# A network piece between the off-diagonal and the state products: a new order of pieces in an HGRN2 + PReLU network kernel

## The chip, the cores and the metric

One core of one Trainium2 chip. The metric is the device time of one execution in microseconds. Before the change three runs took 632.31, 633.37 and 634.52 us; the median is 633.37. A step of such a kernel is made of instructions on five engines that each run in their own order: TensorE (PE; its weight loads are shown apart as PEld), VectorE (DVE), ScalarE (ACT), GpSimd (POOL) and SyncE (SP, which here only starts DMA transfers).

## What is computed

```python
for t in range(S):                                   # HGRN2, for each of B=4 batches and H=8 heads, D=48
    state = f[t, :, None] * state + k[t, :, None] * v[t, None, :]      # f = sigmoid(f_logit)
    y[t] = q[t] @ state
x = y as (B*S, H*D)                                  # 3072 tokens x 384
h = x @ w_in                                         # 384 -> 2048
g = maximum(h, 0) + alpha * minimum(h, 0)
out = g @ w_out                                      # 2048 -> 384
```

All in 32-bit floats; S is 768.

## The kernel before

The sequence is cut into NC = 6 chunks of C = 128 time steps, and the four batches into two pairs. One *step* of the kernel is one chunk of one pair: 12 steps, in the order of `steps` (L725), the chunk being the outer loop. A step's attention gives 256 tokens, which the network then takes in the next step. So step n runs, side by side, the attention of step n, the network of step n−1 and the preparation of step n+1.

Each of these is a generator, and each `yield` ends a *piece*. A string says in which order pieces are issued (L753 to L756): a letter names the generator, a number repeats it.

- `P`, `Q` (`prepare`, L261): the decays of a chunk and the scaled forms of q and k. `P` is this step's own, `Q` the next step's. Five pieces: sigmoid, copies and the lagged products (L282 to L298); four ScalarE copies us<-qd (L317) and VectorE's two scans (L320, L322); q4 and k4 (L324, L350); kh, ks, q3 (L371, L377); the transposed ks and its 16 small DMAs to `ksn` (L404, L430), with f64 (L417). A sixth copies into `A` and starts the DMAs.
- `O` (`carry`, L435): two pieces. The first is the off-diagonal product `off` (64 matmuls, L447; in the first chunk also 128 of L457 and the transposes pk of L474) and ScalarE's copies of it (L465). The second is the state product `pd` (64 matmuls, L487), which takes `ksn` and `vs`, and VectorE's update of the state, `moved(0)` (L497, L501).
- `S` (`attend`, L511): six pieces. For each of the two batches, `raw` (L523) with its four predicated copies (L529) and `qu` (L538) with its seven (L544; three of L560 in the first chunk). Then ScalarE's copies A<-ad for each batch (L566), then `py` (L577), then the second state update, y and the DMAs that make xT of it (L605).
- `n` (`network`, L611): for the step before. Eight pieces of six matmuls `ph` (L620; fp32, which the trace records as 12), ScalarE's `neg` (L625) and VectorE's two `gate` operations (L627); after the fourth and the eighth also four sums (L701). Then pa and pb, pc and pd, pa and pc again, pe, each eight matmuls (L659), and small VectorE operations (L672 to L686) and the stores. The first step's network is plainer: its second product is `po` (L640).
- `a`, `w` and `b`, `v` (`load_weights`, L168): the weights of the two network products arrive in 8 pieces each; the uppers (`a`, `b`) start the load on SP and run two ScalarE operations (L202, L204), the rests (`w`, `v`) four VectorE operations (L210 to L228; for w_out the last one is an accumulating DMA of POOL, L230).
- `W` (L703): sums of w_out's quarters, which the later networks take.

TensorE, VectorE and ScalarE run in exactly the order in which the pieces issue their instructions (L745). SP and POOL are put in order by a scheduler. Two resources tie the engines together: off, pd, raw, qu, py and pk share two PSUM pairs (`psa`, 2 buffers), so each product waits until the copies of the one before the last are done; ph, pa to pe share four banks (`psn`). `neg` has two buffers. The raw weight pieces have four buffers (RAWS), the uppers three (TOPS).

The code that sets the order:

```python
first = (...)          # one string for each of the first four steps
usual = "S n2 S n2 O2 n Q n2 Q n2 Q S3 n Q S n Q n Q n"
```

In a usual step TensorE's order is thus raw qu, ph0 ph1, raw qu, ph2 ph3, off pd, ph4 to ph7, pa pb, py, pc pd, pa pc, pe. (The names `pd` of L487, the state product, and `pd` of L659, a product of the network, are two different things.)

Of the kernel before, what the change touches and what calls it, by code (L numbers as in the profile page):

```python
# [32 lines left out]
def kernel(  # L33
# [39 lines left out]
    W = U * HP * C  # L73
# [61 lines left out]
    for m in range(1, NB):  # L135
        lo = UO[m] + (4 if m == 1 else 0)
        n = NB - m
# [4 lines left out]
    for half in range(2):  # L142
        for m in range(1, NQ):
            n = NQ - m
# [558 lines left out]
    def halves_of_w_out():  # L703
# [20 lines left out]

    steps = [(bp, c) for c in range(NC) for bp in range(B // U)]  # L725
    first = (
        "P2 a P w P a P a w O P w S a w S Q a S O a w S Q2 w S2",
        "P a w a P w n b w n v O b v n b S v n2 P S b S v n b S v n b v n Q b n Q v b O v Q n v W Q S2 Q W n2 W Q W",
        "O n2 S W n2 S Q S n4 O S n Q2 n Q2 S n S n Q n",
        "S n3 S n Q n2 O Q O n2 S Q S n S Q n Q S Q n3",  # L730
    )
    usual = "S n2 S n2 O2 n Q n2 Q n2 Q S3 n Q S n Q n Q n"
    pieces = {key: part for keys, parts in (("aw", load_weights(w_in_sb, w_in, "w_in")),
                                            ("bv", load_weights(w_out_sb, w_out, "w_out")))
              for key, part in zip(keys, parts)}
# [77 lines left out]
```

## Time and profile before

| | before |
|---|---|
| median of three runs | 633.37 us |
| profiled execution | 634.88 us |
| its span | 633.1 us |
| granted TensorE clock, mean | 0.997 |
| TensorE busy | 593.9 us |
| VectorE busy | 512.0 us |
| ScalarE busy | 249.8 us |
| step 3, first raw to next step's | 160.32 to 208.07 us |
| two usual steps, the sixth and seventh | 255.73 to 303.55 and to 351.50 us |

The profile is of one execution. Its chain of work that ended last, and the costliest groups, are read as follows: an operation's line is its place in the kernel, `out<-in` are the program's names of the tiles, the number after x counts records, and for idle time the last part names what ended it.

```profile
PE 73%; DVE 22%; issue 2%; ACT 1%; DMA 1%; DVEq 0%; ACTq 0%
L620 PE MATMUL ph<-xT,w_in_sb 128*128 128x256 f32 x1152 | 258.4, 383 | 0.0
L627 DVE SCALAR_TENSOR_TENSOR gate<-neg,om,ph 128x256 f32<-128x256 f32 x192 | 82.1, 474 | 40.7 <-ACT neg L625 40.5
L566 ACT COPY A<-ad 32x256 f32<-32x256 f32 x96 | 38.5, 401 | 1.4
```

Matmuls are pipelined: the times at which they end are modelled, and a following group can start up to 0.1 us before the end shown for the one ahead of it. "PEldq" in a view stands for TensorE's sequencer, in records of instructions that the engine itself doesn't execute.

### The profile page before, as it was taken

How to read it: one execution, taken by the hardware profiler on the slowest of the kernel's cores; microseconds unless marked ns; L12 is line 12 of the kernel's file. 1: busy time of each engine (PE TensorE's matmuls, PEld its weight loads, DVE VectorE, ACT ScalarE, POOL GpSimd, SP SyncE). 2: the span in 40 equal slices, each digit the busy share in tenths (PEclk: the TensorE clock that was granted, in tenths of full speed). 3: DMA queues.
4: the chain of work that ended last, by engine and by line, in shares of the span. 5: the costliest groups of instructions: out<-in, count | busy, mean ns of one | idle time of the engine just before them, and what ended most of it. 6: DMA issues, size and time to landing. Idle time of an engine off the chain costs nothing.

```text
span 633.1 us, 19007 instructions
## 1 busy us (share of the span) xinstructions
PE 593.9 (94%) x8188; PEld 529.2 (84%) x8188; DVE 512.0 (81%) x1035; ACT 249.8 (39%) x466; POOL 58.8 (9%) x107
## 2 busy tenths in 40 slices
PE   2357999989999999999999999999999999999997
PEld 2356865879789889889889889889889889889997
DVE  5799999999799788888888888888888888762251
ACT  5595792541263153253253253253253253223110
POOL 9010122001001001001001001001001000000000
PEclk9999999999999999999999999999999999999999
DMA  7845796312323313313313313323323301201000
GB/s 239 279 146 182 195 295 162 58 62 73 78 54 91 79 35 85 75 46 84 72 48 84 76 45 84 68 52 84 66 54 85 61 26 26 48 7 26 26 0 26
DMA packets 70323, 53.57 MB, mean 85 GB/s; under 512 B 47296, under 2 KB 62144, under 8 KB 70240
## 3 DMA queue, kind: packets, MB, share of 16 engines
q1 hardware_dynamic: 57536, 25.37, 15.9%
q0 software_dynamic: 7312, 24.78, 13.6%
q10 hardware_dynamic: 5392, 2.21, 1.7%
q8 instruction: 65, 1.06, 0.7%
q14 instruction: 18, 0.15, 0.1%
HBM read 36.21 MB, written 4.72 MB: 65 GB/s over the span
## 4 chain that ended last, share of the span: by engine, by line
PE 73%; DVE 22%; issue 2%; ACT 1%; DMA 1%; DVEq 0%; ACTq 0%
PE ph L620 34%; PE pc L659 8%; PE pa L659 8%; PE pe L659 4%; PE pd L659 4%; PE pb L659 4%; PE qu L538 3%; PE py L577 3%; PE raw L523 3%; PE pd L487 2%; DVE gate L627 2%; DVE S L701 2%; DVE us L333 1%; DVE qd L290 1%; DVE ad L529 1%
## 5 line engine op out<-in xcount | busy, mean ns | idle before, releaser
L620 PE MATMUL ph<-xT,w_in_sb 128*128 128x256 f32 x1152 | 258.4, 383 | 0.0
L620 PEld LDWEIGHTS ph<-xT,w_in_sb 128*128 128x128 f32 x1152 | 216.7, 190 | 32.3 <-issue 2.4
L625 ACT ACTIVATE neg<-ph 128x512 f32<-128x512 f32 x96 | 57.2, 596 | 187.4 <-PE ph L620 139.6
L627 DVE SCALAR_TENSOR_TENSOR gate<-neg,om,ph 128x256 f32<-128x256 f32 x192 | 82.1, 474 | 40.7 <-ACT neg L625 40.5
L659 PE MATMUL pa<-w_out_sb,gate 128*128 128x192 f32 x352 | 62.0, 329 | 1.8 <-DVE gate L627 1.8
L659 PE MATMUL pc<-t,S 128*128 128x192 f32 x352 | 61.7, 329 | 0.0
L659 PEld LDWEIGHTS pa<-w_out_sb,gate 128*128 128x128 f32 x352 | 57.8, 190 | 3.7 <-issue 1.9
L659 PEld LDWEIGHTS pc<-t,S 128*128 128x128 f32 x352 | 57.3, 190 | 0.6
L529 DVE COPY_PREDICATED ad<-mraw,raw 128x256 f32<-128x256 int32 (+1 forms) x96 | 42.3, 441 | 7.3 <-PE raw L523 4.8
L544 DVE COPY_PREDICATED ad<-mquad,qu 128x224 f32<-128x224 int32 (+6 forms) x140 | 41.9, 299 | 6.2
L422 ACT COPY A<-q 48x512 f32<-48x512 f32 x44 | 27.2, 617 | 42.4 <-DVE q L371 38.4
L566 ACT COPY A<-ad 32x256 f32<-32x256 f32 x96 | 38.5, 401 | 1.4
L333 DVE TENSOR_TENSOR us<-us,fs 128x768 f32<-128x768 f32 (+5 forms) x60 | 36.7, 612 | 0.1
L677 ACT COPY o<-pa 128x192 f32<-128x192 f32 x11 | 3.5, 318 | 75.3 <-PE pa L659 61.5
L290 DVE TENSOR_TENSOR qd<-qd,f 128x768 f32<-128x768 f32 (+2 forms) x36 | 27.1, 753 | 6.1 <-ACT qd L285 6.1
L538 PE MATMUL qu<-us,k 48*32 48x112 f32 (+1 forms) x1536 | 27.1, 259 | 4.2 <-issue 3.0
L701 DVE TENSOR_TENSOR S<-gate 128x512 f32<-128x512 f32 x44 | 30.3, 688 | 0.8
L659 PE MATMUL pe<-w_out_sb,S 128*128 128x192 f32 x176 | 30.5, 327 | 0.3 <-ACT o L677 0.3
L659 PE MATMUL pb<-t,gate 128*128 128x192 f32 x176 | 30.4, 326 | 0.0
L659 PE MATMUL pd<-w_out_sb,S 128*128 128x192 f32 x176 | 30.4, 326 | 0.0
L577 PEld LDWEIGHTS py<-A,vs 128*64 128x64 f32 x768 | 25.7, 145 | 5.5 <-issue 2.8
L577 PE MATMUL py<-A,vs 128*64 128x64 f32 x768 | 28.1, 233 | 2.0 <-ACT vs L503 1.0
(110 smaller groups left out, 743.0 us busy)
## 6 DMA issues: line engine op xcount, KB each, us to landing
w_out_raw<-in_w_out SPq DMA_DIRECT2D x8, 767.8 KB, 5.0
w_in_raw<-in_w_in SPq DMA_DIRECT2D x8, 767.2 KB, 7.1
f<-in_fT POOLq DMA_DIRECT2D x11, 512.0 KB, 4.5
q<-in_qT POOLq DMA_DIRECT2D x11, 512.0 KB, 4.2
k<-in_kT POOLq DMA_DIRECT2D x11, 512.0 KB, 4.6
out<-o SPq DMA_DIRECT2D x24, 192.0 KB, 2.1
vs<-in_v POOLq DMA_DIRECT2D x22, 192.0 KB, 4.3
w_out_sb<-w_out_lead POOLq DMA_DIRECT2D x8, 384.0 KB, 6.3
```

What stands on the lines that cost most here:

```text
L290: nc.vector.tensor_tensor(qdv[d], qdv[d - 1][:, :, :, 1:5 - d], f[:, :, 1:5 - d].rearrange("p (g i) r -> p g i r", i=NB), ALU.mult)
L333: nc.vector.tensor_tensor(us[:, :, UO[m]:UO[m] + 4 * n].rearrange("p g (i r) -> p g i r", r=4), us[:, :, skip:skip + 4 * n].rearrange("p g ...
L529: nc.vector.copy_predicated(adu[:, :, :, d:4], mraw[:, d, :, d:4].bitcast(I32).unsqueeze(1).broadcast_to((128, H, NB, n)), rv[:, :, QO[d]: ...
L538: nc.tensor.matmul(qu[DB * j:DB * (j + 1), par, hp * QS + 4:hp * QS + QL], lhsT=k4[r_, g * DB:(g + 1) * DB], rhs=us[r_, g, 4:QL], start=Tr ...
L544: nc.vector.copy_predicated(ad[:, u, :, :, 4 * m:DB], mquad[:, lo:lo + n].bitcast(I32).unsqueeze(1).unsqueeze(1).broadcast_to((128, 2, HP, ...
L566: nc.scalar.copy(A[s_, u, :, s_], ad[s_, u].rearrange("p r h t -> p (r h) t"))
L577: nc.tensor.matmul(py[64 * par:64 * par + 64, u, o:o + CH], lhsT=vs[bp][:, cc, u, hd * D:hd * D + 64], rhs=A[:, u, par * HP + hp, CH * cc: ...
L620: nc.tensor.matmul(ph[:, j * T:(j + 1) * T], lhsT=w_in_sb[:, kt, m * 128:(m + 1) * 128], rhs=xT[:, kt], start=(kt == 0 and j == 0), stop=( ...
L625: nc.scalar.activation(neg, phv, AF.Relu, scale=-1.0)
L627: nc.vector.scalar_tensor_tensor(gate[:, m % NH, m // NH], neg[:, j], om[:, m:m + 1], phv[:, j], ALU.mult, ALU.add)
L659: nc.tensor.matmul(to[:, 0:DH], lhsT=of(f), rhs=by(f), start=(f == 0 and not more), stop=(f == NH - 1), skip_group_check=True)
L701: nc.vector.tensor_tensor(to, x_, y_, op)
```

## The change

Only the strings change. No instruction is added or removed on TensorE or VectorE.

```diff
     first = (
-        "P2 a P w P a P a w O P w S a w S Q a S O a w S Q2 w S2",
-        "P a w a P w n b w n v O b v n b S v n2 P S b S v n b S v n b v n Q b n Q v b O v Q n v W Q S2 Q W n2 W Q W",
-        "O n2 S W n2 S Q S n4 O S n Q2 n Q2 S n S n Q n",
-        "S n3 S n Q n2 O Q O n2 S Q S n S Q n Q S Q n3",
+        "P2 a P w P a P2 a w a w O a w S2 Q O S Q w S a Q S w S",
+        "P n b P a w a n O b w2 v2 S P b n3 v S b2 S2 v2 n Q b n2 Q O b v b n v2 n v S W Q2 S Q W n Q W n W",
+        "n2 S n W n3 S n2 Q O S n O Q2 S n S Q S n Q2 n2",
+        "S n2 S Q n2 O n O S2 n3 Q2 S n2 S Q n Q n2 Q",
     )
-    usual = "S n2 S n2 O2 n Q n2 Q n2 Q S3 n Q S n Q n Q n"
+    usual = "S n2 S n O n O n Q n3 Q n Q S3 n Q S n Q n Q n"
```

In a usual step two things move:

- The first piece of `O` (off) goes ahead of ph3, and the second (pd) behind it. Before, off and pd followed each other behind ph3.
- The second piece of `Q` (ScalarE's us<-qd copies and VectorE's scans) goes from between ph6 and ph7 to behind ph7 and its sums.

In the first steps all kinds of pieces move. In step 0 the attention's pieces come in pairs and weight pieces spread otherwise; in step 1 the prepare pieces come before weight pieces, the first network piece before the uppers of w_in, and off before the second; in step 2 the network's first pieces come ahead of off; in step 3 a network piece stands between off and pd, which were adjacent on TensorE before. With this the scheduler's orders on SP and POOL change up to there: the first load of w_out comes ahead of the last two of w_in, and loads of k, f and v change places with the accumulating DMAs of w_out.

## The prediction

> **What bounds the kernel now.** I read the page's busy shares and slices first, then the windows cut at the steps' ends, the waits of TensorE, the chain through one usual step, and the timeline of TensorE around the two products that the change moves.
>
> ```profile
> PE 593.9 (94%) x8188; PEld 529.2 (84%) x8188; DVE 512.0 (81%) x1035; ACT 249.8 (39%) x466; POOL 58.8 (9%) x107
> PE   2357999989999999999999999999999999999997
> DVE  5799999999799788888888888888888888762251
> ```
>
> TensorE is full from the fifth slice to the end; VectorE is full in slices three to ten, the start-up. The windows say the same in microseconds (busy time and record count of each engine; the stretches are start-up, steps 1 and 2, one usual step, and the end):
>
> ```profile
> 0.00:62.50 62.50, 31.71 (x847) 27.27 (x849) 50.22 (x94) 38.81 (x62) 20.46 (x53) 1.00 0.66 213
> 62.50:160.32 97.82, 94.33 (x1316) 76.83 (x1304) 94.59 (x180) 50.31 (x89) 13.89 (x18) 0.98 0.52 140
> 303.55:351.50 47.95, 47.84 (x660) 43.37 (x660) 41.36 (x86) 17.95 (x36) 3.39 (x5) 1.00 0.27 67
> 590.40:633.10 42.70, 39.33 (x211) 36.55 (x209) 14.46 (x31) 5.42 (x10) 0.00 (x0) 1.00 0.05 17
> ```
>
> A usual step is 47.84 of 47.95 us TensorE, with VectorE at 41.36. So a usual step gets shorter only if TensorE's own stream does. The waits that TensorE shows lie in the start-up, except a few:
>
> ```profile
> PE off L447 <- DVE q L371: 12.1, 1, 12.1
> PE off L457 <- issue: 4.8, 1, 4.8
> PE off L457 <- DVE us L407: 3.4, 2, 2.8
> PE pa L659 <- DVE gate L627: 1.8, 1, 1.8
> ```
>
> What the waits don't show is inside the busy time. The chain through a usual step (start, length, records), where off and pd follow each other:
>
> ```profile
> 317.95 0.71 PE off L447 x50
> 318.66 0.05 issue
> 318.71 0.72 PE pd L487 x6
> 319.43 0.04 issue
> 319.47 0.89 PE pd L487 x57
> 320.35 10.56 PE ph L620 x48
> ```
>
> Six matmuls of pd take as long as the other 57. Elsewhere in the same run, where pd stands behind a network piece, and where off stands alone before one:
>
> ```profile
> 109.83 0.76 PE L447 MATMUL off<-q,kh 48*32 48x32 f32 x64
> 110.51 5.45 PE L620 MATMUL ph<-xT,w_in_sb 128*128 128x256 f32 x24
> 135.32 0.94 PE L487 MATMUL pd<-vs,ksn 64*48 64x48 f32 x64
> ```
>
> pd is 0.94 us there. The records of pd's line in a usual step name what else it runs:
>
> ```profile
> L487 PEldq EVENT_SEMAPHORE  x9: 51/51/51, 318.4 to 319.4; - x9
> ```
>
> Nine semaphore instructions of 51 ns on TensorE's sequencer, at 318.4 to 319.4, exactly the slow microsecond. In the stretch 133 to 137, around the quick pd, the same view has none: its sequencer had passed them while network matmuls ran.
>
> [...]
>
> **The usual step, part by part.** Nothing is added or removed; TensorE's order goes from "ph2 ph3 off pd ph4" to "ph2 off ph3 pd ph4". Before, from off's start to ph4's start: 320.28 − 317.88 = 2.40 us. After, off alone is 110.51 − 109.83 = 0.68, and pd alone 0.94 less the modelled tail of about 0.07 plus a changeover of about 0.05, some 0.92. Together 1.60; saved 0.80. From pd's start to the next ph the eight usual steps have 1.54, 1.51, 1.57, 1.51, 1.55, 1.54, 1.68 and 1.58, so this step is typical. For cover: ph3 runs 2.66 us and pd's semaphores need 9 × 0.051 = 0.46. Bounds: nothing saved if the sequencer doesn't get ahead through one piece, 0.95 if off too gets cheaper. I take 0.75 for each of eight steps: −6.0.
>
> Waits that could appear. off now comes a network piece earlier and needs the PSUM pair that raw1 had; VectorE's copies of raw1 (L529) end at 314.13 and off would start at 315.2: 1.1 us to spare. pd needs qu1's pair, free at 316.53, and starts at 318.6. VectorE's gate 3 moves 0.7 later; it stood idle 1.37 us before that gate, and behind it wait the sums of L701, moved(0) and gate 4. It then has 0.75 idle before L290 and 2.04 before L672 to absorb it. Behind off's ScalarE copies (1.27) stands neg3, which isn't ready for 2.7 us.
>
> Second, Q's scans (L320, L322) and ScalarE's four us<-qd copies (2.15) go behind gate 7 and neg7. Gate 7 was at 332.58, behind both scans; now it is about 0.7 us sooner against ph7, and pa (2.93 instead of 2.76 us, a wait of 0.17 in seven steps) needn't wait: between 0 and −1.2 for all, I take −0.5. The sums that pc needs end sooner too. The us<-qd copies end at about 332.8, before pa's copy and the 3.33 us of A<-ad copies that py needs, so those don't move. The orders of SP's and POOL's queues change only up to the loads and stores of the first steps; in the usual steps each transfer keeps its place.
>
> **The first four steps.** I replayed the new lists by hand with the durations of before's rows. Step 0: VectorE waited 3.75 us for raw0 at 30.15; a weight piece (L210 to L228, 2.6) now lies there, and the attend copies end at about 37.9 instead of 39.4. In ScalarE's order the second A<-ad copy falls behind an upper pair (1.8), so y stays at about 47.0 and ph0 with it: no gain yet on TensorE, 1.5 less backlog on VectorE. Step 1: the prepare pieces come ahead of weight pieces, so the 2.81 us wait of L457 goes and pk ends near 62.2 instead of 64.8. What is late next is raw0: it needs off's pair, and ScalarE does neg0, one w_out upper, two w_in uppers and neg1 before off's copies; about 2.0 lost. Then gates before po 0.35, and landings of w_out pieces 0.5. The po end comes at 108.0 instead of 109.85. Moved queue entries count: the first w_out load goes to SP ahead of the last two w_in loads (median landing 7.1 us), whose uppers stand ahead of neg1; POOL's k load for step 2 goes ahead of a w_out accumulate. Step 2: the 1.77 us gate wait before pa goes, because the scans no longer stand in front, but VectorE is the bound there (94.59 of 97.82), and I find 0.8 and 0.7 us of waits for it early in step 3. Ahead at the end of step 2: about 2.2. Bounds: 5 gained if VectorE's idle is all filled, 4 lost if an upper arrives late in step 1. In step 3 off and pd were adjacent as well (1.58); separated, −0.75.
>
> Sum: −6.0 − 0.5 − 2.2 − 0.75 = −9.45 us. The profiled execution was 634.88 (span 633.1), 1.5 above the median of 633.37; it would come to 625.4. From the median: 623.9. A replay by hand forgets small waits rather than inventing them, so I give back 0.6: 624.5.
>
> **Rivals.** (a) Separation saves nothing in usual steps: pd is slow because of its shape change behind off, or the sequencer stops at the semaphores all the same. Against it stand 0.94 in step 2 and the clean split of 6 and 57 matmuls. Left would be −2.2 − 0.5: 630.7. (b) The usual steps gain, the start-up gives 3 to 4 us back in place of gaining: ScalarE's in-order queue in step 1, or w_out pieces landing late. For it: VectorE at 97%, no slack. 633.4 − 7.25 + 2.5, about 628.5. (c) Slower: off waits for VectorE's copies of raw1 in every usual step. The price is what they are late beyond 1.1 us; from 2.25 us late (1.1 + 9.2/8) it eats everything, and at 2.7 late it gives 8 × 1.6 − 9.2 = +3.6: 637.0. For it: VectorE runs from 341.26 through the next step's raw1 copies with one gap of 1.08. Against it: that gap is there, and nothing is put into that stretch.
>
> **How the numbers follow.** Forecast 0.70, (a) 0.10, (b) 0.14, (c) 0.06. The range reaches from 620.0 (start-up 5 gained, pa's wait all gone) to 629.6, which takes in most of (b) and leaves out (a) and (c). About 1.9 us, 0.3%, is what a measurement can tell from no change. (a) and (b) are mostly beyond it on the fast side; a little of each isn't. Faster 0.90, within 0.04, slower 0.06.
>
> **What would show it.** In the changed profile: off start to ph start near 0.7, pd near 0.94 with no semaphore instruction inside it, usual steps of about 47.0; pa at 2.76; no L407 wait; ph4 of step 3 about 3 us sooner. Wrong if pd stays near 1.6, if a wait of off for L529 appears, or if the first usual step begins after 208.

## The result, and the profile after

The changed kernel takes 630.9 us in the median (628.54 to 633.09), the kernel before 633.41 (632.15 to 635.04) on the same chip: a ratio of 0.996, interval 0.995 to 0.997. It is faster, by 2.5 us; forecast were 8.9. The profiled execution took 629.98 (span 628.2), 0.9 below its median, while that of before was 1.5 above its own: spans differ by more than medians do.

The page of the kernel after, busy shares, and slices of the clock that TensorE was granted:

```profile
PE 590.1 (94%) x8188; PEld 525.2 (84%) x8188; DVE 512.1 (82%) x1035; ACT 248.7 (40%) x466; POOL 58.5 (9%) x107
...
PEclk9958799999999999999999999999999999999999
```

TensorE's busy time fell by 3.8 us. By the trace's clock records the clock is at half from 32.8 to 49.9 us and from 60.1 to 70.3 us. The kernel before shows a 9 in all slices, but its clock records begin only at 52.59 us, and ahead of them its rows are as slow as at half (the figures stand in the last section); behind them it is at half from 62.8 to 66.2 us. So the second stretch is the one that differs, 10.2 us against 3.4. TensorE's waits, kernel after:

```profile
PE off L457 <- issue: 5.5, 2, 3.8
PE py L577 <- ACT A L566: 4.2, 5, 1.9
...
PE pe L659 <- ACT o L677: 2.4, 1, 2.4
...
PE ph L620 <- DMA xT<-y: 0.9, 1, 0.9
PE off L457 <- DVE us L407: 0.6, 1, 0.6
```

The wait for L407 has shrunk from 3.4 to 0.6 as forecast and the gate wait of pa is gone; a wait of pe in step 2 and one for xT were not in the forecast. Of py's 4.2 us, 3.7 lie in step 0, where the copies A<-ad were forecast to come late, and 0.45 in the first usual step; shorter stops of py in the other usual steps don't appear in this list. Two rows of a usual step of TensorE in the kernel before, then the same step in the kernel after:

```profile
330.75 2.93 PE L659 MATMUL pa<-w_out_sb,gate 128*128 128x192 f32 x16
336.21 2.15 PE L577 MATMUL py<-A,vs 128*64 128x64 f32 x64
```

```profile
313.78 0.76 PE L447 MATMUL off<-q,kh 48*32 48x32 f32 x64
314.46 2.86 PE L620 MATMUL ph<-xT,w_in_sb 128*128 128x256 f32 x12
317.25 0.94 PE L487 MATMUL pd<-vs,ksn 64*48 64x48 f32 x64
318.11 10.63 PE L620 MATMUL ph<-xT,w_in_sb 128*128 128x256 f32 x48
328.58 2.76 PE L659 MATMUL pa<-w_out_sb,gate 128*128 128x192 f32 x16
331.18 2.76 PE L659 MATMUL pb<-t,gate 128*128 128x192 f32 x16
333.87 2.44 PE L577 MATMUL py<-A,vs 128*64 128x64 f32 x64
336.24 2.87 PE L659 MATMUL pc<-t,S 128*128 128x192 f32 x16
```

pd is 0.94 us, and its nine semaphore instructions now run under the network piece, as the records of its line in this stretch say. One of them waits 0.475 us, and ph3 covers that too:

```profile
L487 PEldq EVENT_SEMAPHORE  x9: 51/51/475, 314.4 to 315.8; - x9
```

From the second raw to ph4 it is 318.11 − 309.30 = 8.81 us, against 320.28 − 310.73 = 9.55 before: 0.74 saved in this step. (These are times from start to start. The ends shown overlap the next start by more than the 0.1 us said above: raw at 309.30 lasts 0.92, and qu starts at 309.99.) The mean of the eight usual steps is 8.88 against 9.50, 0.62 saved. pa takes 2.60 from start to start instead of 2.76. But py takes 2.37 instead of 2.07. Sum −0.60; the step is 47.33 instead of 47.95. The mean of seven usual steps is 47.37, before 47.83. ScalarE shows why py got longer, first in the kernel before, then in the same stretch of the kernel after:

```profile
328.85 2.15 ACT L317 COPY us<-qd 128x256 f32<-128x256 f32 x4
331.00 0.60 ACT L625 ACTIVATE neg<-ph 128x512 f32<-128x512 f32 x1
333.93 3.33 ACT L566 COPY A<-ad 32x256 f32<-32x256 f32 x8
```

```profile
329.18 0.60 ACT L625 ACTIVATE neg<-ph 128x512 f32<-128x512 f32 x1 [2.39 <-DVE gate L627]
329.68 2.16 ACT L317 COPY us<-qd 128x256 f32<-128x256 f32 x4
331.63 0.37 ACT L667 COPY Csum<-pa 128x192 f32<-128x192 f32 x1
331.90 3.33 ACT L566 COPY A<-ad 32x256 f32<-32x256 f32 x8
```

Gates 5, 6 and 7 on VectorE, kernel after:

```profile
328.20 2.48 DVE L627 SCALAR_TENSOR_TENSOR gate<-neg,om,ph 128x256 f32<-128x256 f32 x6
```

The neg row in each of the two blocks above is neg7. In the kernel after ScalarE is idle for 2.39 us ahead of it, and the view names a gate as what ended that. Most of this is TensorE's own time, as ph7 ends, by the model, only at 318.11 + 10.63 = 328.74; the gate's share is some 0.4 us, from there to 329.18. `neg` has two buffers, and gate 5, the first of these three, must free one. The copies us<-qd now stand behind neg7, and the A<-ad copies behind them end at 335.23: py's records stop inside its second batch, from 334.92 to 335.28, for the last of them. In the kernel before, neg7 starts at 331.00, right behind ph7, which ends at 320.28 + 10.63 = 330.91.

### The profile page after: what moved, and what is told of

It reads as the page before. It is cut to its first block, busy times and chain, and to the rows that moved or that the text cites. A ratio compares the mean times of both kernels' runs of the same rounds, so it can differ in the third digit from the quotient of the medians.

```text
span 628.2 us, 19015 instructions
## 1 busy us (share of the span) xinstructions
PE 590.1 (94%) x8188; PEld 525.2 (84%) x8188; DVE 512.1 (82%) x1035; ACT 248.7 (40%) x466; POOL 58.5 (9%) x107
## 3 DMA queue, kind: packets, MB, share of 16 engines
q8 instruction: 65, 1.06, 0.8%
## 4 chain that ended last, share of the span: by engine, by line
PE 64%; DVE 17%; ACT 10%; issue 4%; DMA 3%; ACTq 1%; DVEq 0%; SPq 0%
PE ph L620 26%; PE pc L659 9%; PE pa L659 6%; PE pe L659 5%; PE pd L659 5%; PE qu L538 3%; ACT A L566 3%; PE raw L523 3%; DVE S L701 3%; DVE gate L627 3%; DVE qd L290 3%; PE py L577 2%; ACT us L317 2%; DMA xT<-y 2%; PE po L640 2%
## 5 line engine op out<-in xcount | busy, mean ns | idle before, releaser
L620 PE MATMUL ph<-xT,w_in_sb 128*128 128x256 f32 x1152 | 262.2, 385 | 0.9 <-DMA xT<-y 0.9
L529 DVE COPY_PREDICATED ad<-mraw,raw 128x256 f32<-128x256 int32 (+1 forms) x96 | 42.3, 441 | 3.1 <-PE raw L523 0.6
L659 PEld LDWEIGHTS pe<-w_out_sb,S 128*128 128x128 f32 x176 | 28.8, 190 | 2.7 <-ACT o L677 2.7
```

What stands on the lines that cost most here:

```text
L529: nc.vector.copy_predicated(adu[:, :, :, d:4], mraw[:, d, :, d:4].bitcast(I32).unsqueeze(1).broadcast_to((128, H, NB, n)), rv[:, :, QO[d]: ...
L620: nc.tensor.matmul(ph[:, j * T:(j + 1) * T], lhsT=w_in_sb[:, kt, m * 128:(m + 1) * 128], rhs=xT[:, kt], start=(kt == 0 and j == 0), stop=( ...
L659: nc.tensor.matmul(to[:, 0:DH], lhsT=of(f), rhs=by(f), start=(f == 0 and not more), stop=(f == NH - 1), skip_group_check=True)
```

## The experiments

All times are medians, each kernel beside runs of the kernel before on the same chip (633.4 to 634.2 there). "Steps 0 to 3" are the four strings of `first`.

**The two halves of the change.** e1 takes from the change's diff only the line of `usual`, e2 only the four of `first`.

> The first four orders of before, the usual order of the change. Theory A (the usual steps gain 0.5 us each net: 0.7 from the separated state product less about 0.3 of py waiting for the copies A<-ad; the start-up gave back): 629.4, that is 4.0 below before. Rival (the usual order's gain needs the new first steps too, or the usual order also carries the loss): 631 or more.

> The first four orders of the change, the usual order of before. Theory A: the new first steps lose 0 to 2 us, 633.4 to 635, since medians left 1.5 us unaccounted for after 8 x 0.5. Rival (start-up is neutral or better, as the one profile with step 4 beginning 0.9 us sooner says): 632.5 or less. The granted clock should fall below 0.99 if the new start-up is what lowers it.

e1: 629.62, ratio 0.9939 (0.9922 to 0.9955). e2: 635.11, ratio 1.0019 (1.0008 to 1.003). So the usual steps gain 4.0 us, and the first four lose 1.5.

**The two halves of the usual step.**

e3 sets only off and pd apart, e4 only puts the second prepare piece later; both against before:

```diff
-    usual = "S n2 S n2 O2 n Q n2 Q n2 Q S3 n Q S n Q n Q n"
+    usual = "S n2 S n O n O n Q n2 Q n2 Q S3 n Q S n Q n Q n"
```

```diff
-    usual = "S n2 S n2 O2 n Q n2 Q n2 Q S3 n Q S n Q n Q n"
+    usual = "S n2 S n2 O2 n Q n3 Q n Q S3 n Q S n Q n Q n"
```

> The first steps of before; in the usual string only off and pd are set apart by a network piece, the scans and us<-qd copies stay ahead of the eighth network piece. Theory A (moving that piece behind neg7 is what made py wait): 8 x 0.75 = 6.0 below before, 627.4, with py at 2.15 us and pd at 0.94. Rival (py waits just the same because TensorE got ahead of ScalarE): as the usual order alone, about 629.4.

> The first steps of before; in the usual string only the second prepare piece moves behind the eighth network piece; off and pd stay adjacent. Theory A: py waits about 0.3 us per step, pa gains 0.17, pd stays at 1.6: 0 to +1.5 against before, 633.4 to 635. Rival (the sooner gate7 is a gain): 632.2 or less.

e3: 634.09, ratio 1.0009 (0.9995 to 1.0022); e4: 632.96, ratio 0.9991 (0.998 to 1.0003). Both expectations missed. Neither half alone gains much, together they gain 4.0. In e4 the copies us<-qd stand behind neg7 as well, and py still takes 2.07 or 2.08 in six of seven usual steps: neg7 starts at 330.94, right behind ph7, which ends at 320.22 + 10.63 = 330.85. So the new place of these copies makes py wait only where TensorE has got ahead of gate 5. The timeline of TensorE in e3, where pa is cut in two:

```profile
318.45 0.94 PE L487 MATMUL pd<-vs,ksn 64*48 64x48 f32 x64
...
329.78 2.44 PE L659 MATMUL pa<-w_out_sb,gate 128*128 128x192 f32 x14
332.79 0.59 PE L659 MATMUL pa<-w_out_sb,gate 128*128 128x192 f32 x2 [0.57 <-DVE gate L627]
333.22 2.76 PE L659 MATMUL pb<-t,gate 128*128 128x192 f32 x16
```

pd is quick, and pa's last product waits 0.57 us for gate 7: pa takes 3.44 from start to start instead of 2.76, and the gain is spent. VectorE has as much to do as before. off in front of ph3 puts gate 3 later, 8.82 us behind the step's second raw instead of 7.94; VectorE's idle time ahead of L290, 0.75 us, is used up by that, and gate 7 starts 21.85 us behind the second raw in both kernels. So VectorE is no later than before, but it doesn't follow the earlier TensorE.

**The cause of the slow pd, and the place of off.** e6 keeps before's orders and takes away what pd waits for; from the second chunk on it leaves the keys out of the state:

```diff
-  lhsT=ksn[s_, u, hp * 128 + 64 * par:hp * 128 + 64 * par + D],
+  lhsT=(ident[s_, 64 * par:64 * par + D] if c else ksn[s_, u, hp * 128 + 64 * par:hp * 128 + 64 * par + D]),
```

> Before with one edit: from the second chunk on, the state product takes its stationary operand from the constant identity tile in place of ksn, so it no longer waits for the 16 transfers of ksn; off and pd stay adjacent. It leaves out the keys' part of the state, in every step but the first two. Theory S (the nine semaphore instructions make pd slow behind off): pd about 0.94 us, two or fewer semaphore instructions. Rival (the change of tile shape behind off does): pd stays at 1.6 us. The time: no gain, since gate7 behind the scans then holds pa by about 0.6, 633 to 634.5; if the time falls by 4 or more, VectorE's gate7 wasn't the next limit.

626.75, ratio 0.9889 (0.9868 to 0.9911). The timeline of e6, and its records of pd's line from 312 to 318:

```profile
314.26 0.76 PE L447 MATMUL off<-q,kh 48*32 48x32 f32 x64
314.95 0.94 PE L487 MATMUL pd<-vs,ident 64*48 64x48 f32 x64
315.81 10.63 PE L620 MATMUL ph<-xT,w_in_sb 128*128 128x256 f32 x48
```

```profile
L487 PEldq EVENT_SEMAPHORE  x1: 51/51/51, 314.8 to 314.8; - x1
```

Directly behind off, in the same tile shape, pd takes 0.94 us once eight of nine semaphore instructions are gone; with `ksn` and all nine it takes 0.94 in the kernel after, behind a network piece. So neither the shape nor the operand makes pd slow, but the semaphore instructions where nothing long covers them. The expectation of its time was wrong: it fell by 7.4, so gate 7 behind the scans isn't a limit in itself. Two kernels with before's first strings test two remedies. v1 takes the new usual order and puts the first batch's A<-ad copies ahead of ph7; v2 takes before's, leaves off behind ph3 and puts only pd one network piece later, which also puts gate 4 ahead of moved(0) on VectorE:

```diff
-    usual = "S n2 S n O n O n Q n3 Q n Q S3 n Q S n Q n Q n"
+    usual = "S n2 S n O n O n Q n2 S n Q n Q S2 n Q S n Q n Q n"
```

```diff
-    usual = "S n2 S n2 O2 n Q n2 Q n2 Q S3 n Q S n Q n Q n"
+    usual = "S n2 S n2 O n O Q n2 Q n2 Q S3 n Q S n Q n Q n"
```

> The first steps of before; the change's usual order with the first batch's copies A<-ad moved ahead of the eighth network piece, into ScalarE's 2.4 us wait for neg's second buffer. Theory A (py's 0.3 us wait is ScalarE being late behind us<-qd): py back to 2.1 us, 8 x 0.3 = 2.4 better than the usual order alone, 627.2. Rival (another wait, such as gate7 or the second batch's copies, takes its place): 629 or more.

> The first steps of before; in the usual order off stays behind the fourth network piece and only pd goes one network piece later (off, fifth piece, pd); the scans stay ahead of the eighth piece. Theory G (e3 gained nothing because off ahead of the fourth piece made gate3, and with it VectorE's chain up to gate7, 0.7 us later): with gate3 in its old place pa doesn't wait, py doesn't either, 8 x 0.75 = 6 below before, 627.5. Rival (pa waits for gate7 wherever off is, unless the scans move): 632 or more.

v1: 627.58, ratio 0.9899 (0.9882 to 0.9915), its usual steps 46.85 to 47.28. v2: 628.1, ratio 0.9911 (0.9892 to 0.993), its usual steps 46.98 to 47.16. The timeline of v2:

```profile
314.09 0.76 PE L447 MATMUL off<-q,kh 48*32 48x32 f32 x64
314.78 2.86 PE L620 MATMUL ph<-xT,w_in_sb 128*128 128x256 f32 x12
317.56 0.94 PE L487 MATMUL pd<-vs,ksn 64*48 64x48 f32 x64
...
326.30 2.77 PE L659 MATMUL pa<-w_out_sb,gate 128*128 128x192 f32 x16
328.91 2.76 PE L659 MATMUL pb<-t,gate 128*128 128x192 f32 x16
331.61 2.15 PE L577 MATMUL py<-A,vs 128*64 128x64 f32 x64
```

pd, pa and py are all quick, with the scans where before had them; gate 7 starts 20.95 us behind the second raw, 0.9 sooner than in e3. So the gain doesn't need the scans moved where gate 3 keeps its place. How much of this is gate 3's and how much gate 4's new place was not tried apart.

**The first steps one by one**, each the new string of one step with the other three of before and the new `usual`; the measure is e1's 629.62.

> The change's usual order and its order of step 0 alone; steps 1 to 3 as before. Against the usual order alone (629.6). Theory B (step 0's order brings the first network piece 2.4 us sooner, and half of it lasts through the VectorE-bound steps 1 and 2): 628.4. Rival (the landings and VectorE take it all back in step 1): 629.6.

> The change's usual order and its order of step 1 alone. Theory B (raw0 straight behind pk waits for ScalarE's copies of off, and the second network piece behind it then runs at the reduced clock): about 1 us worse than the usual order alone, 630.6. Rival (step 1 is neutral, the loss is step 2's): 629.6.

> The change's usual order and its order of step 2 alone. Theory B (the copy o<-pa stands behind five transfers that ScalarE starts, and pe waits 2.4 us for it; the first network piece waits 0.9 us for xT): 2 to 3 us worse than the usual order alone, 632. Rival (VectorE sets the end of step 2 anyway, so the wait costs nothing): 629.6.

> The change's usual order and its order of step 3 alone. If parts add up: 630.9 for the changed kernel = 629.6 + 1.35 (step 0) + 1.8 (step 1) - 1.2 (step 2) + step 3, so step 3's share is about -0.7: 628.9. Rival (off and pd apart in step 3 meet VectorE as in the usual steps and gain nothing): 629.6.

m0: 630.97 (+1.35), ratio 0.9956 (0.994 to 0.9973). m1: 631.43 (+1.8), 0.9961 (0.9943 to 0.9978), with a wide spread, 627.84 to 636.1, whose cause is open. m2: 628.46 (−1.2), 0.992 (0.9901 to 0.9938). m3: 628.71 (−0.9), 0.9923 (0.9902 to 0.9944). Theory B missed in m0 and m2. Each interval overlaps that of e1, so a single share is uncertain by about 1 us; added to e1 the four give 630.7, and the changed kernel has 630.9. As far as these medians tell, steps 0 and 1 lose, steps 2 and 3 gain. pe's wait in step 2 costs nothing net, as m2 isn't slower than e1; that VectorE sets the end of that step was not shown apart.

**What steps 0 and 1 lose by.** Step 0 of m0, timeline of TensorE ("issue" is time in which it waited for nothing that the profile shows):

```profile
20.09 0.98 PE L457 MATMUL off<-us 48*32 48x16 f32 x79 [0.55 <-DVE us L407]
26.18 0.71 PE L457 MATMUL off<-us 48*32 48x16 f32 x49 [5.11 <-issue]
26.82 1.97 PE L474 MATMUL pk<-ident,ks 128*128 128x128 f32 x8
28.72 1.22 PE L523 MATMUL raw<-qd,k 48*32 48x80 f32 x64
29.95 0.29 PE L538 MATMUL qu<-us,k 48*32 48x52 f32 x6
32.02 0.77 PE L538 MATMUL qu<-us,k 48*32 48x52 f32 x58 [1.77 <-issue]
32.61 1.18 PE L523 MATMUL raw<-qd,k 48*32 48x80 f32 x64
33.98 0.39 PE L538 MATMUL qu<-us,k 48*32 48x52 f32 x5 [0.19 <-DVE ad L560]
35.55 1.01 PE L538 MATMUL qu<-us,k 48*32 48x52 f32 x59 [1.19 <-issue]
```

TensorE stops in the middle of a row. From stop to stop it is 49 + 8 + 64 + 6 = 127 records, then 58 + 64 + 5 = 127: with their weight loads 254 instructions. A stretch of that length is called a block here. The pages of both kernels list a queue q8 of kind "instruction" with 65 packets and 1.06 MB, 16.3 KB each.

The trace has the start and length of each packet. In m0 packets of this queue run from 23.62 to 24.72, from 29.66 to 30.60 and from 33.15 to 34.15, and TensorE goes on at 26.18, 32.02 and 35.55, each time 1.4 or 1.5 us behind the packet's end. In the 20 profiled runs 41 stops of 1 us or more stand at the same counts of recorded matmuls and weight loads (446, 700, 954, 1208, 1717 and 1971 ahead of them, to within two), whatever the order of pieces, and each ends 1.2 to 1.6 us behind such a packet. So these stops are waits for instructions. Both orders of step 0 have them: the first takes 3.6 to 5.1 us in each of the 16 profiled runs with IDLE = 40.

In the changed step 1, off, L457, pk, raw and qu follow each other without a network piece, and it stops twice there:

```profile
56.54 0.97 PE L457 MATMUL off<-us 48*32 48x16 f32 x94
59.17 0.41 PE L457 MATMUL off<-us 48*32 48x16 f32 x34 [1.66 <-issue]
...
65.06 0.84 PE L538 MATMUL qu<-us,k 48*32 48x52 f32 x43 [2.04 <-issue]
65.83 10.24 PE L620 MATMUL ph<-xT,w_in_sb 128*128 128x256 f32 x36
```

The three network pieces behind it take 10.24 us instead of the 8.04 of other places, as the clock is at half up to 70.3. m1's profile, of one of its quicker executions (629.35), has neither stop in step 1, and these pieces take 10.11 there as well.

x1 is the changed kernel with more small matmuls at the start; m0x and e1x are m0 and e1 with the same edit; w1 is the changed kernel with large matmuls filling step 1.

```diff
-IDLE = 40
+IDLE = 56
```

```diff
         if not c:
+            for _ in range(7 if bp else 0):
+                nc.tensor.matmul(off[:, 0, 384:512], lhsT=ident, rhs=ones[:, 0:128], start=True, stop=True)
...
             qu = pair(f"qu{u}_{i}")
+            for _ in range(5 if bp and not c and u == 0 else 0):
+                nc.tensor.matmul(qu[:, 0, 0:256], lhsT=ident, rhs=ones[:, 0:256], start=True, stop=True)
```

> The changed kernel with 56 in place of 40 small matmuls at the very start: 32 matmul records and as many weight loads more ahead of everything. Theory C ([...]): the stop inside L457 of step 0, now behind its 79th record, comes behind its 47th, and the stop inside L457 of step 1, now behind the 94th, behind the 62nd. Rival (a data wait): both stay where they are. Time within the changed kernel's own spread, 628.5 to 633.

> The changed kernel with twelve extra large matmuls in step 1, whose results are overwritten or not read: seven (about 1.8 us) ahead of L457 and five (about 2.2 us) ahead of the first qu. Theory C (in step 1 TensorE stops for its instructions and then runs at a lower clock[...]): the stops of 1.7 and 2.0 us go, the clock recovers sooner, 629 to 631, no worse than the changed kernel's 630.9. Rival (the stops are waits for data that the profile doesn't name, and fillers only add): 633 to 635.

> As m0_first0 (630.97), with 56 in place of 40 small matmuls at the start. Theory C (step 0's loss is TensorE stopping for instructions, 5.1 us inside L457 of step 0 and 2.9 inside that of step 1): the stops go and with them the loss, 629.6 or less. Rival (step 0's order loses by ScalarE's and VectorE's order): 630.5 to 631.5 as before.

> As e1_usual_alone (629.6; first steps of before, the change's usual order) with 56 in place of 40 small matmuls at the start. Theory C (the instruction supply was the loss of step 0's order, so that order is itself a gain once supplied, as in m0x at 627.2): here less than the 3.7 us that m0 gained, 628 to 629.6. Rival (the extra matmuls help any order by the same, and step 0's order stays about 1 us worse): 626 or less.

x1: 630.28, in its only run; the stops didn't move as expected, both of L457 vanished, and raw of step 1 waits for ScalarE instead, 2.54 us:

```profile
57.33 1.25 PE L457 MATMUL off<-us 48*32 48x16 f32 x128
...
62.15 1.34 PE L523 MATMUL raw<-qd,k 48*32 48x80 f32 x64 [2.54 <-ACT A L465]
```

A wait for data would have stayed. The packets say why the first stop went. The packet for the block behind the 446th record starts only when TensorE has come to the block before, at the 192nd: 3.4 to 5.0 us behind that record with IDLE = 40, 1.4 to 1.7 with 56. With 40 that record stands behind TensorE's wait of 12 us for q (L371), with 56 ahead of it, at 7.25 us; so x1's packet lands at 9.92 us, the changed kernel's at 23.22. Yet x1's time is within the changed kernel's spread, and three network pieces of its step 1 take 10.09 us without a stop ahead of them.

m0x: 627.24, ratio 0.9891 (0.987 to 0.9912), 3.7 below m0. e1x: 628.56, ratio 0.9907 (0.9886 to 0.9929), 1.1 below e1. In the profile of m0x no stop of 1 us is left at those counts; in that of e1x the first is gone, but stops of 2.27, 2.75 and 1.67 us stand at the next three. So what step 0 lost in m0 was its instruction supply. That its order is itself a gain of 1.3 when supplied is not clear of the noise, as the intervals of m0x and e1x overlap. w1: 630.4, ratio 0.9948 (0.9928 to 0.9969): with about 4 us of extra work it is no slower than the changed kernel, the two stops of step 1 shrink to 0.54 and 0.34 us, its windows show a clock of 1.00 from 56 to 84 us, and the network pieces take their 8.04 again:

```profile
67.66 8.04 PE L624 MATMUL ph<-xT,w_in_sb 128*128 128x256 f32 x36
```

How much of step 1's 1.8 us is the stops, how much the clock and how much something else was not separated; x1 and m1, which lack the stops there, say that they aren't all of it.

**A better version.** best_mix has steps 0 and 1 of before, 2 and 3 of the change, and v1's usual order; best2 the same with v2's; best3 is best_mix with the new step 0 and IDLE = 56.

> Orders of steps 0 and 1 from before, of steps 2 and 3 from the change, and the usual order with the first batch's copies ahead. If parts add up: 627.6 (that usual order) - 1.2 (step 2's order) - 0.75 (off and pd apart in step 3) = 625.7. Rival (VectorE-bound steps absorb one of them): 627 or more.

> Orders of steps 0 and 1 from before, 2 and 3 from the change, and the usual order with only pd one piece later. If theory G holds and parts add up: as best_mix, 625 to 625.7. Rival: the usual order with the copies ahead remains the better, 626.5 or more here.

> best_mix (625.3) with the change's order of step 0 and 56 small matmuls at the start. If m0x's 627.2 against the usual order alone at 629.6 carries over: 622.9. Rival (VectorE-bound steps 1 and 2 take it back): 625 or more.

best_mix: 625.27, ratio 0.9872 (0.9849 to 0.9896). best2: 626.62, ratio 0.9892 (0.9866 to 0.9918), with intervals that overlap. best3: 622.57, ratio 0.982 (0.9797 to 0.9843): 11 us below before, faster than both kernels.

## Why the prediction was wrong, point by point

- **The slow pd.** Right in cause, as e6 shows: nine semaphore instructions, which in the kernel after the sequencer passes from 314.4 to 315.8 us, beside a network piece that starts at 314.46 and ahead of pd's start at 317.25. The size was a little high: 0.75 us per step forecast, 0.62 measured in the mean (0.74 in the step shown). Rival (a) didn't occur.
- **pa.** Right in cause: it waits no more, 0.13 per step in the mean, about 1.1 for eight where 0.5 was taken.
- **"The us<-qd copies end at about 332.8, before pa's copy and the 3.33 us of A<-ad copies that py needs, so those don't move."** This step failed. They did move against TensorE, and py took 0.30 us more in the step shown, 0.29 in the mean, some 2.3 of the 6.5 us that the usual steps were to gain. The prediction let VectorE's idle time "absorb" gate 3's 0.7 us. It did: from the second raw to gate 5 it is 328.20 − 309.30 = 18.90 us after, 329.69 − 310.73 = 18.96 before. But TensorE itself was now ahead, and gate 5 wasn't: from ph4's start to gate 5 it is 328.20 − 318.11 = 10.09 us after, 329.69 − 320.28 = 9.41 before. neg7 needs gate 5's buffer, and the moved us<-qd copies stand behind neg7. The two buffers of `neg` were in the code and not in the sum. The parts give 8 × (0.62 + 0.13 − 0.29) = 3.7 us; e1 has 4.0. In v1 and v2 py doesn't wait (2.02 and 2.08 us), and they gain 2.0 and 1.5 us over e1.
- **The new place of the scans.** Priced as a small gain beside the main one. With off ahead of ph3 it is a condition of it: without it, e3 gains nothing.
- **Step 3.** It fits: −0.75 forecast, −0.9 in m3, uncertain by about 1 us; pd of that step takes 0.94 instead of 1.58 there.
- **"Step 1: ... The po end comes at 108.0 instead of 109.85", and 2.2 ahead at the end of step 2.** This step failed. By the medians step 0 loses 1.35, step 1 loses 1.8, step 2 gains 1.2, that is 2.0 lost where 2.2 gained was forecast. In the profiled executions po is over at 109.61, and step 3's first network piece starts at 161.99 instead of 161.60 before. (In the kernel before the first raw of step 3 starts at 158.60, not at 160.32 as the table has it; in the kernel after it starts at 160.31.) The first usual step begins at 207.15, 0.9 sooner than before, where 2.2 + 0.75 was forecast. The replay used the durations of before's rows for rows that stood in another order. But TensorE's "issue" gaps, 4.8 us in the first wait view, were known and were treated as fixed; they depend on which rows fall at the ends of the instruction blocks and on when these land. For step 0 m0x shows that this was the loss; what step 1 lost by stays open between the stops, the clock at half and other waits. The predicted stall of raw0 behind ScalarE's queue, 2.0 us, shows in x1, 2.54; in the changed kernel raw0 waits only 0.37, behind a stop.
- **The waits of step 2.** pe behind o<-pa (2.4 us) was missed: ScalarE starts five transfers ahead of that copy. It cost nothing net (m2).
- **The rivals.** (b) came closest, a start-up that gives back; but in it the usual steps gain 7.25 us, and they gained 4.0. Of its mechanism, ScalarE's queue shows in x1; TensorE's waits in the changed kernel have no late landing of a w_out piece. (c) didn't occur: no wait of off for L529 appears in a usual step.

## What to carry to other kernels

A busy TensorE can hide time: where the same row takes 0.94 us in one place and 1.6 in another, look at its sequencer's semaphore records, and put a row of long matmuls ahead of an instruction with many waits. When a piece is put ahead of another, follow the one that is put back through every engine to its buffers: a delay that is "absorbed" by idle time is absorbed only from that idle time on. A time that is absorbed there still counts against an engine that has meanwhile become faster. A replay from durations doesn't hold where TensorE waits for its instructions, here 1 to 5 us at a time: where a row stops in its middle for nothing that the profile names, look at the packets of the instruction queue.

## What was not expected of the hardware

- TensorE stopped 1 to 5 us at ends of blocks, 254 recorded instructions apart, in rows of small matmuls, until 1.2 to 1.6 us after the next block's packet was over. Sixteen more small matmuls at the very start were worth 3.7 us in one order and 1.1, within the noise, in another.
- A 9 for the clock in a start-up needn't be a full clock. The clock records of the kernel before begin at 52.59 us and those of e1 at 51.22; ahead of these times both pages show 9, but the 12 records of xt (L595) take 4.88 us from start to start at 48.10 and 5.25 at 45.85. In m1, whose record has full clock from 44.33 us on, they take 2.67; in the kernel after, at half by its record for the first 3.9 us of them, 4.59. So mean clocks of one kernel can differ with little difference in speed: of the kernel before, 46 executions with a mean below 0.99 have a median of 634.0 us, 61 others 633.4, which the spread doesn't tell apart. The clock records of the kernel before and of the kernel after hold two values, 1.0 and 0.5; what sets them is shown by no run. Where the half falls on full network pieces, as in step 1 of the changed kernel, three of them took 2.2 us more.
